# First heads' rows by way of DRAM, a rounded last key block, and a probability store in quarters

## The chip, the core and the metric

The kernel runs on one core of one Trainium2 chip. The metric is device time in microseconds (us) for one execution. A core has five engines that run their own instruction streams in order: TensorE (PE in the profile; its weight loads are PEld), VectorE (DVE), ScalarE (ACT), GpSimd (POOL) and SyncE (SP). SP here only issues DMAs, and ScalarE can issue some too. An engine goes past an instruction only when the semaphores it waits for have come, so a DMA that waits in SP's stream holds every DMA behind it.

## The reference, cut to what matters

```python
def _attn_ref(q, k, v, f):                     # (4, 8, 576, 64), f (4, 8, 576)
    scores = scale * np.matmul(q, k.transpose(0, 1, 3, 2))
    cum = np.cumsum(np.log(np.clip(f, 0.0001, 1.0)), axis=-1)
    decay = cum[:, :, :, None] - cum[:, :, None, :]
    scores = np.where(causal, -1000000000.0, scores + decay)
    attn = softmax(scores)
    return np.matmul(attn, v)

x = _attn_ref(q, k, v, f) as (2304, 512)       # heads side by side
h = np.maximum(x @ w_in, 0.0);  x = h * h @ w_out          # 512 -> 2048 -> 512
h = x @ w_in2;  out = (h - np.tanh(h)) @ w_out2            # 512 -> 2048 -> 512
```

## The kernel before, in words

There are 32 heads of 576 positions. A head's queries are cut into five tiles (64, then four of 128), its keys into five blocks of 128, 128, 128, 128 and 64. Values are kept as float32r (a rounded float32 that TensorE multiplies in one pass) in a high part and a low rest, so a product is made of two or three one-pass matmuls. A plain float32 matmul stands in the trace as two matmul instructions.

The cumulated log of `f` enters the scores as four extra rows of the contraction: rows 64 to 67 of the tile `QB`, beside the low parts of q and k. `setup` (L213) computes them (`chl`), stores them to the DRAM tensor `aug_d`, and loads the first eight heads' rows from there. The first head's rows alone go from `chl` straight to SBUF by four small DMAs of ScalarE (L245).

The heads run in four forms. `first_a` (L440) does the first 320 positions of heads 0 to 7 before any of the MLP, and takes the first weights along: `fetch_w` loads one 1 MB piece, `split_a` and `split_b` turn it into high and low float32r parts (L144 on ScalarE, L145, L146 and L122 on VectorE, L109 on ScalarE). The tables `SPLIT_A` and `SPLIT_B` say after which head which piece is split. `first_b` does the rest of these heads beside the first MLP block. Heads 8 to 15 (`attention`, L654) are transposed on TensorE. Heads 16 to 31 are laid out slot by slot by `plan_head` (L754): the probabilities are transposed in 32x32 squares by VectorE (`turn`) into `T`, stored to DRAM (`put`), loaded back in the wanted order as `PTl` (`get`), split into a high part `PTh` on ScalarE (`p_high`) and a low rest on VectorE (`p_low`), and multiplied with the values `VH` (`pv_begin`, `pv_end`). A slot is half an MLP step; in a slot, what is planned "behind" comes after the matmuls.

In `pv_parts` (L574) the key blocks 0 to 3 use the split values `VH` and split probabilities. The last 64 keys (block 4, L602) and the corner (the first 64 queries, L609) are plain float32 matmuls with the raw values `VR`.

```python
        seq = [(hi, 0), (hi, 1), (lo, 1), (hi, 2), (lo, 2), (hi, 3), (lo, 3), (None, 4), (lo, 0)]
                if pt is None:
                    nc.tensor.matmul(po4, vr[0:rows, 4], p4, start=False, stop=False)
```

The order within each engine up to the third MLP block comes from a scheduler that works by a timeline; after it, from the order in which the code is written.

Of the kernel before, what the change touches and what calls it, by code (L numbers as in the profile page):

```python
# [44 lines left out]
}  # L45
FETCH = {6: 4, 7: 5, 8: 6}
SPLIT_A = {4: 0, 6: 1, 8: 2, 9: 3}
SPLIT_B = {5: 0, 7: 1, 9: 2, 10: 3}
# [15 lines left out]
YSEQ = (0, 6, 1, 7, 2, 3, 4, 5)  # L64
PT_SZ = (64, 256, 384, 512, 576)
# [3 lines left out]
def kernel(  # L69
# [143 lines left out]
    def setup():  # L213
# [15 lines left out]
        for a in (0, 1):  # L229
            nc.vector.memset(A_QB[0][64:68, 0, a].bitcast(F32), (-1.0, 1.0)[a])  # L230
# [21 lines left out]
        for k in (0, 1, 2):  # L252
            n = min(3, H - 3 * k)
            j = int(k == 0)
            for a in (0, 1):
                queued(A_QB[k][64:68, j:, a].bitcast(F32), aug_d[3 * k + j:3 * k + n, :, a, :320].rearrange("h r s -> r h s"))
        with tc.issue_after(latest(EngineType.SP)):
            fetch_w(w1, 0, 0)
        first_load((6, 7))
        for k in (1, 2, 3):  # L260
            with tc.issue_after(latest(EngineType.SP)):
                fetch_w(w1, k, k)
# [24 lines left out]
    def load_v(u):  # L287
        VR[u] = two.tile([128, 5, D], F32, tag="VR", bufs=2, name="VR")
        src = v[u] if u < UT else v[u].rearrange("(b i) c d -> i b (c d)", b=4)
        nc.sync.dma_start(VR[u], src)  # L290

    def prep_v(u):
        VH[u] = one.tile([128, 4, 2, D], F32R, tag="VH", name="VH")
        rounded(by(pre(u) + "vh"), VH[u][:, :, 0], VR[u][:, 0:4])
        rest(by(pre(u) + "vl"), VH[u][:, :, 1], VR[u][:, 0:4], VH[u][:, :, 0])
# [28 lines left out]
    def first(h, part):  # L324
# [3 lines left out]
        if part:  # L328
            tag = ("R", "QA", "QA")[h % 3]
            r = (one if tag == "R" else two).tile([128, 2, S], F32, tag=tag, name="R0")  # L330
            vr = two.tile([128, 5, D], F32, tag="VR", bufs=2, name="VR")
# [108 lines left out]
    def first_a(also):  # L440
        st = {}
        WARM.append(psh.tile([128, 512], F32, tag="h", name="warm"))
        for h in range(H + 3):
            if h < H:
# [8 lines left out]
                if h + 3 < H:  # L453
                    with tc.issue_after(latest(EngineType.DVE)), tc.issue_after(latest(EngineType.Pool)):
                        first_prep([h + 3])
# [80 lines left out]
    def trans(u, t):  # L536
# [11 lines left out]
        if t == 1:  # L548
            rounded(by("ptr"), PT["t"][0:64, :, 3, 1], ps[0:64, 256:384].rearrange("p (q j) -> p q j", q=4))
            rounded(by("ptr"), PT["t"][0:64, 2:4, 3, 0], ps[0:64, 384:448].rearrange("p (q j) -> p q j", q=2))  # L550

    def turn(t):
        p, T = P[t], PT["t"]
        if t == 0:
            nc.vector.transpose(T[0:64, 0:2, 3, 0], p[0:64, :64].rearrange("p (b j) -> p b j", b=2))
# [7 lines left out]
    def put(u):  # L565
        by("put").dma_start(p_d[u % 2], PT["t"].rearrange("p b a s j -> p (b a s j)"))
# [7 lines left out]
    def pv_parts(u):  # L574
        vh, vr = VH.pop(u), VR.pop(u)
# [3 lines left out]
        if u < UT:  # L579
            hi, lo = (PT[k].rearrange("p q a s j -> p (q a s j)").rearrange("p (c t j) -> p c t j", c=4, t=4) for k in "hl")  # L580
            po = ps.rearrange("p (s j) -> p s j", s=4)
            at = lambda p, c, t: p[:, c, t:]
            rows = 64
            po4, p4 = ps[0:64, 384:512].rearrange("p (q j) -> p q j", q=4), PT["t"][0:64, :, 3, 1]
            po_at = lambda t: po[:, t:]
            p0 = PT["t"][0:64, 2:4, 3, 0]
        else:
            hi, lo = PT["h"], PT["l"]
            po = ps.rearrange("p (q s j) -> p q s j", q=4, s=4)
            at = lambda p, c, t: p[:, :, c, t:]  # L590
# [938 lines left out]
```

## Time and profile before

| | us |
|---|---|
| median of 3 runs (lowest to highest) | 1013.88 (1013.79 to 1014.28) |
| the profiled execution | 1015.15 |
| its span, first to last instruction | 1013.4 |
| TensorE matmuls busy, in the span | 990.9 (98%) |
| VectorE / ScalarE / GpSimd busy | 706.9 / 608.6 / 381.3 |

The profile comes from one execution. Busy time is the time that an engine has an instruction under way. A matmul that is issued and held up counts as busy, so a lengthened row shows what the idle time does not. The granted clock of TensorE is given as a share of 2.4 GHz: 1.00 and 0.50 are its two levels here.

### The profile page before, as it was taken

To read this page: it belongs to the slowest core of one execution; us is meant where nothing else is said; L and a number is where in the kernel's file an instruction comes from. 1 tells how busy PE (TensorE), PEld (TensorE's weight loads), DVE (VectorE), ACT (ScalarE), POOL (GpSimd) and SP (SyncE) were. 2 spreads that over 40 slices of the span, in tenths; PEclk is the share of its full clock that TensorE was granted. 3 is DMA by queue.
4 is the path that set the end of the run, shared out by engine and by line. 5 is a ranking of instruction groups with operands and counts; after the bars stand their busy time and mean duration, and the time that the engine had idled before them with its cause. 6 is when DMAs were issued, how large, how long until landed. Compare 5 with 4: busy or idle time off the path is not lost.

```text
span 1013.4 us, 19745 instructions
## 1 busy us (share of the span) xinstructions
PE 990.9 (98%) x7120; PEld 930.6 (92%) x7120; DVE 706.9 (70%) x1675; ACT 608.6 (60%) x1347; POOL 381.3 (38%) x453
## 2 busy tenths in 40 slices
PE   7979999999999999999999999999999999999998
PEld 7767678888999899998999999999999999999998
DVE  5886675777676777675825668477777787877851
ACT  4886676766776667676746777456556553333330
POOL 3453455555543324343402456247456520000000
PEclk8999999999999999999999999999999999999999
DMA  8545542223556556665547984997776699434451
GB/s 265 233 139 189 182 155 81 98 80 112 213 217 230 203 209 208 224 219 187 196 150 250 357 290 172 367 381 254 282 271 249 235 343 343 147 118 135 139 167 63
DMA packets 84529, 211.54 MB, mean 209 GB/s; under 512 B 8440, under 2 KB 33072, under 8 KB 80080
## 3 DMA queue, kind: packets, MB, share of 16 engines
q1 hardware_dynamic: 84304, 210.28, 59.2%
q8 instruction: 56, 0.92, 0.4%
q14 instruction: 41, 0.34, 0.1%
q10 hardware_dynamic: 128, 0.01, 0.0%
HBM read 132.20 MB, written 78.05 MB: 207 GB/s over the span
## 4 chain that ended last, share of the span: by engine, by line
PE 77%; DMA 8%; DVE 6%; ACT 3%; issue 2%; POOL 2%; SPq 1%; DVEq 0%; ACTq 0%; POOLq 0%
PE yp L193 17%; PE hp L164 17%; PE wp L1270 16%; PE wp L1194 11%; PE o_ps L605 4%; PE wp L1282 2%; DMA raw<-in_w_dram 2%; DMA R<-in_qk_dram 2%; DMA g_d<-gq 2%; PE o_ps L406 1%; DMA PTl<-p_d 1%; DVE wt L966 1%; PE s_ps L698 1%; PE t_ps L541 1%; PE s_ps L697 1%
## 5 line engine op out<-in xcount | busy, mean ns | idle before, releaser
L164 PE MATMUL hp<-xhl,w 128*128 128x288 f32 x1536 | 236.3, 299 | 2.5 <-POOL xhl L122 1.0
L164 PEld LDWEIGHTS hp<-xhl,w 128*128 128x128 f32 x1536 | 213.1, 189 | 7.8 <-issue 1.8
L193 PE MATMUL yp<-gh,w 128*128 128x288 f32 x1024 | 212.8, 299 | 0.0
L193 PEld LDWEIGHTS yp<-gh,w 128*128 128x128 f32 x1024 | 164.4, 188 | 3.1 <-issue 2.1
L1194 PE MATMUL wp<-xo,wg 128*128 128x288 f32 x1152 | 159.9, 296 | 2.0 <-DVE gq L1201 1.9
L1270 PE MATMUL wp<-go,wg 128*128 128x256 f32 x1344 | 161.4, 283 | 0.0
L1270 PEld LDWEIGHTS wp<-go,wg 128*128 128x128 f32 x1344 | 161.4, 192 | 0.0
L1194 PEld LDWEIGHTS wp<-xo,wg 128*128 128x128 f32 x1152 | 155.0, 188 | 3.5 <-DVE gq L1201 3.4
L193 PE MATMUL yp<-gl,w 128*128 128x288 f32 x512 | 151.5, 297 | 0.0
L517 POOL TENSOR_SCALAR P<-P,ST 128x448 f32<-128x448 f32 (+4 forms) x120 | 83.4, 704 | 136.6 <-DVE ST L713 83.0
L109 ACT ACTIVATE go<-gt 128x1792 fp32r<-128x1792 f32 (+1 forms) x34 | 58.3, 1717 | 101.2 <-PE wp L1270 79.9
L497 DVE CUSTOM_DVE_ANT_0 P<-s_ps,mk 128x320 f32<-128x320 f32 (+3 forms) x151 | 63.5, 438 | 72.6 <-PE s_ps L698 41.5
L506 ACT ACTIVATE P<-P,ST 128x320 f32<-128x320 f32 (+4 forms) x151 | 84.8, 562 | 47.3 <-DVE ST L497 45.2
L193 PEld LDWEIGHTS yp<-gl,w 128*128 128x128 f32 x512 | 96.4, 188 | 0.8 <-issue 0.8
L122 DVE TENSOR_TENSOR gl<-tmp,gh 128x288 fp32r<-128x288 f32 x96 | 58.6, 611 | 51.6 <-ACT tmp L174 51.1
L122 DVE TENSOR_TENSOR go<-gt,go 128x1792 fp32r<-128x1792 f32 (+1 forms) x34 | 69.6, 2048 | 34.9 <-ACT go L109 32.0
L170 ACT ACTIVATE tmp<-hp 128x288 f32<-128x288 f32 x128 | 52.0, 406 | 63.1 <-PE hp L164 62.2
L122 POOL TENSOR_TENSOR wt<-wt,whi 128x512 f32<-128x512 f32 (+1 forms) x48 | 60.7, 1286 | 59.2 <-ACT whi L109 28.8
L174 ACT ACTIVATE tmp<-tmp 128x288 f32<-128x288 f32 x128 | 56.7, 443 | 3.4
L173 ACT ACTIVATE gh<-tmp 128x288 fp32r<-128x288 f32 x128 | 56.1, 438 | 1.9
L1201 DVE TENSOR_TENSOR gq<-wp,sm 128x288 f32<-128x288 f32 x96 | 40.8, 453 | 17.0 <-ACT sm L1200 11.3
L1245 DVE TENSOR_TENSOR gt<-gt 128x256 f32<-128x256 f32 x128 | 49.4, 428 | 1.5 <-DMA gt<-g_d 0.4
(171 smaller groups left out, 1673.7 us busy)
## 6 DMA issues: line engine op xcount, KB each, us to landing
wg<-wg_d SPq DMA_DIRECT2D x24, 896.0 KB
g_d<-gq SPq DMA_DIRECT2D x32, 576.0 KB
raw<-in_w_dram SPq DMA_DIRECT2D x16, 1024.0 KB
p_d<-T SPq DMA_DIRECT2D x16, 1024.0 KB
PTl<-p_d SPq DMA_DIRECT2D x64, 256.0 KB
raw<-in_w_dram SPq DMA_DIRECT2D x32, 512.0 KB
gt<-g_d SPq DMA_DIRECT2D x32, 512.0 KB
R<-in_qk_dram SPq DMA_DIRECT2D x24, 576.0 KB
```

The source lines that it names most:

```text
L109: eng.activation(out, in_, AF.Copy)
L122: eng.tensor_tensor(out, in_, hi.bitcast(F32), ALU.subtract)
L164: nc.tensor.matmul(ps, w[:, k * 128:(k + 1) * 128], x[:, k], start=(jj == 0), stop=(jj == 11))
L170: nc.scalar.activation(tmp, ps, AF.Relu)
L173: nc.scalar.activation(gh, tmp, AF.Square)
L174: nc.scalar.activation(tmp, tmp, AF.Square)
L193: nc.tensor.matmul(yp[m][:, :n], w[:, c], x, start=(at == 0 and j == 0), stop=(at == NF - 1 and j == 2))
L497: nc.vector.tensor_tensor_reduce(p[:rows, a:b], ps[:rows, :b - a], mk[:rows, o:o + b - a], -0.125, 3.0e38 if mn is None else mn, ALU.add, ...
L506: nc.scalar.activation(p[:rows, :n], p[:rows, :n], AF.Exp, bias=mn, scale=-1.0, accum_out=st[:rows, 1, t:t + 1])
L517: by(n_by).tensor_scalar(p[:rows, :n], p[:rows, :n], st[:rows, 3, t:t + 1], 1.0, ALU.mult, ALU.mult)
L1194: nc.tensor.matmul(ps, wg[:, ws, k * 128:(k + 1) * 128], xo[:, xs, k], start=(i == 0 and first_), stop=(i == 5), skip_group_check=True)
L1270: nc.tensor.matmul(ps, wg[:, ws, m * 128:(m + 1) * 128], YO[n][xs][:, YX[xn]], start=(j == 0 and m == 0 and i == 0), stop=(j == 2 and i == ...
```

## The change

Six things are edited. (1) The extra rows of head 0 are no longer written to SBUF directly: `chl` is stored to `aug_d` by two DMAs of ScalarE instead of SyncE, and the rows of heads 0 to 2, 3 to 5 and 6 to 7 are loaded from there, each group in front of a weight piece. (2) `SPLIT_A` and `SPLIT_B` split the first weight pieces after earlier heads. (3) Block 4 of the keys is split like the others (`VH` has five blocks), and so is the corner. (4) The raw values have one buffer instead of two, loaded after the values of the head before are split. (5) `put` stores four quarters of 512 columns. (6) `get` is planned one slot earlier, behind the matmuls.

```diff
-    "ptr": "V", "pth": "A", "ptl0": "V", ...
+    "pth": "A", "pth3": "A", "ptl0": "V", ...
-SPLIT_A = {4: 0, 6: 1, 8: 2, 9: 3}
-SPLIT_B = {5: 0, 7: 1, 9: 2, 10: 3}
+SPLIT_A = {1: 0, 4: 1, 7: 2, 9: 3}
+SPLIT_B = {2: 0, 5: 1, 8: 2, 10: 3}
+LOW = (0, 0, 0, 1)
@@ setup
-        for r in (0, 1):
+        nc.scalar.dma_start(aug_d[:, 0:2, 0], chl.bitcast(F32))
+        nc.scalar.dma_start(aug_d[:, 2:4, 1], chl.bitcast(F32))
+        def aug(k, put):
+            n = min(3, H - 3 * k)
             for a in (0, 1):
-                p = 64 + 2 * a + r
-                nc.scalar.dma_start(A_QB[0][p:p + 1, 0, a].bitcast(F32), chl[0:1, r, :320].bitcast(F32))
-        queued(aug_d[:, 0:2, 0], chl.bitcast(F32))
-        queued(aug_d[:, 2:4, 1], chl.bitcast(F32))
+                put(A_QB[k][64:68, :, a].bitcast(F32), aug_d[3 * k:3 * k + n, :, a, :320].rearrange("h r s -> r h s"))
         first_load((4,))
+        aug(0, queued)
+        early(0)
...
+        aug(1, queued)
         first_load((5,))
...
@@ load_v, prep_v
-        VR[u] = two.tile([128, 5, D], F32, tag="VR", bufs=2, name="VR")
+        VR[u] = two.tile([128, 5, D], F32, tag="VR", bufs=1, name="VR")
-        VH[u] = one.tile([128, 4, 2, D], F32R, tag="VH", name="VH")
+        VH[u] = one.tile([128, 5, 2, D], F32R, tag="VH", name="VH")
@@ trans
-            rounded(by("ptr"), PT["t"][0:64, :, 3, 1], ps[0:64, 256:384].rearrange("p (q j) -> p q j", q=4))
-            rounded(by("ptr"), PT["t"][0:64, 2:4, 3, 0], ps[0:64, 384:448].rearrange("p (q j) -> p q j", q=2))
+            rounded(nc.scalar, eh, ps[0:64, 256:448])
+            rest(nc.vector, el, ps[0:64, 256:448], eh)
@@ put
-        by("put").dma_start(p_d[u % 2], PT["t"].rearrange("p b a s j -> p (b a s j)"))
+        for b in range(4):
+            by("put").dma_start(p_d[u % 2][:, 512 * b:512 * b + 512], PT["t"][:, b].rearrange("p a s j -> p (a s j)"))
@@ pv_parts
-        seq = [(hi, 0), (hi, 1), (lo, 1), (hi, 2), (lo, 2), (hi, 3), (lo, 3), (None, 4), (lo, 0)]
-        if u >= UT:
-            seq = [(hi, 0), (hi, 1), (hi, 2), (hi, 3), (None, 4), (lo, 1), (lo, 2), (lo, 3), (lo, 0)]
+            seq = [(hi, 0), (hi, 1), (lo, 1), (hi, 2), (lo, 2), (hi, 4), (hi, 3), (lo, 3), (lo, 4), (lo, 0)]
+            seq = [(hi, 0), (hi, 1), (hi, 2), (hi, 3), (hi, 4), (lo, 1), (lo, 2), (lo, 3), (lo, 4), (lo, 0)]
-            nc.tensor.matmul(ps0[0:64, 0:64], vr[0:rows, 0], p0, start=True, stop=True)
+            for n, (a, p) in enumerate(((0, hi), (1, hi), (0, lo))):
+                nc.tensor.matmul(ps0[0:64, 0:64], vh[0:rows, 0, a], p0(p), start=(n == 0), stop=(n == 2))
@@ p_high, p_low
-        s0 = max(0, c - 1)
+        s0 = LOW[c]
@@ plan_head
-            plan(o + 7, get, k)
+            plan(o + 6, get, k, behind=True)
```

At the start, SyncE's stream before (`R` is a head's raw q and k, `V` the values, `raw` a weight piece) was:

```order
L211 DMA R_135<-in_qk_dram 128x2x320
L211 DMA aug_d<-chl 32x2x576 x2
L211 DMA R_166<-in_qk_dram 128x2x320
L211 DMA V_168<-in_v_dram 128x8x192
L211 DMA R_166<-in_qk_dram 128x2x320
L211 DMA QB_142<-aug_d 4x2x320 x2
L211 DMA QB_143<-aug_d 4x3x320 x2
L211 DMA QB_144<-aug_d 4x2x320 x2
L134 DMA raw<-in_w_dram 128x2048
```

and is now:

```order
L212 DMA R_135<-in_qk_dram 128x2x320
L212 DMA R_160<-in_qk_dram 128x2x320
L338 DMA R_728<-in_qk_dram 64x1152
L212 DMA QB_142<-aug_d 4x3x320 x2
L135 DMA raw<-in_w_dram 128x2048
L212 DMA V_166<-in_v_dram 128x8x192
L212 DMA QB_143<-aug_d 4x3x320 x2
L212 DMA R_160<-in_qk_dram 128x2x320
L135 DMA raw<-in_w_dram 128x2048
```

The `chl` stores have left SyncE, the first weight piece has moved up from behind all the rows to right behind those of the first three heads.

ScalarE's stream in the same stretch (`QA<-R` are heads 0, 1 and 2, then more; `P,ST` is an exponential of head 0) was:

```order
L109 ACTIVATE QA_188<-R_132 128x640 x2
L109 ACTIVATE QA_197<-R_135 128x640
L245 DMA QB_142<-chl 1x16x20 x4
L265 ACT_TABLE_LOAD
L265 ACTIVATE wrk<-wrk 32x1
L109 ACTIVATE QA_197<-R_135 128x640
L109 ACTIVATE QA_291<-R_166 128x640 x2
L506 ACTIVATE P_241,ST<-P_241,ST 128x320
```

and is now:

```order
L110 ACTIVATE QA_182<-R_132 128x640 x2
L110 ACTIVATE QA_191<-R_135 128x640
L267 ACT_TABLE_LOAD
L267 ACTIVATE wrk<-wrk 32x1
L241 DMA aug_d<-chl 32x2x576
L242 DMA aug_d<-chl 32x2x576
L145 ACTIVATE raw<-raw 128x1024
L512 ACTIVATE P_235,ST<-P_235,ST 128x320
```

The stores stand behind the table load, and the first step on the first weight piece stands in front of head 0's first exponential, where three heads' `QA` stood.

In a head of the last form that closes a pair, SyncE's stream was:

```order
L566 DMA p_d_83<-T 128x2048
L489 DMA x_d_81<-xsh 128x576
L490 DMA x_d_81<-xs 128x576
L572 DMA PTl<-p_d_83 32x4x512 x4
L269 DMA R<-in_qk_dram 128x1152
```

and is now:

```order
L572 DMA p_d_83<-T 128x512 x4
L578 DMA PTl<-p_d_83 32x4x512 x4
L495 DMA x_d_81<-xsh 128x576
L496 DMA x_d_81<-xs 128x576
L271 DMA R<-in_qk_dram 128x1152
```

The load of `PTl` has moved ahead of the two stores of the attention output, and there are four stores of a quarter each. Load b waits for the store of quarter b.

## Rows read from the trace of the kernel before

**Rows 1.** The page, busy time of each engine in the span.

```profile
PE 990.9 (98%) x7120; PEld 930.6 (92%) x7120; DVE 706.9 (70%) x1675; ACT 608.6 (60%) x1347; POOL 381.3 (38%) x453
```

**Rows 2.** TensorE in order of time, a head of the last form: start, length, line, operation.

```profile
264.78 0.43 PE L193 MATMUL yp<-gh,w 128*128 128x288 f32 x2
...
266.40 0.91 PE L605 MATMUL o_ps<-PTh,VH 128*128 128x512 f32 x4
267.24 0.43 PE L602 MATMUL o_ps<-PTl,VR 128*64 128x128 f32 x2
267.60 1.85 PE L164 MATMUL hp<-xhl,w 128*128 128x288 f32 x12
269.29 0.92 PE L605 MATMUL o_ps<-PTl,VH 128*128 128x512 f32 x4
...
270.39 0.53 PE L193 MATMUL yp<-gh,w 128*128 128x288 f32 x2
```

**Rows 3.** TensorE in order of time, a head of the form before it.

```profile
172.18 0.28 PE L605 MATMUL o_ps<-PTl,VH 128*128 128x256 f32 x1
...
172.75 0.49 PE L605 MATMUL o_ps<-PTl,VH 128*128 128x512 f32 x1
...
173.43 1.85 PE L164 MATMUL hp<-xhl,w 128*128 128x288 f32 x12
```

**Rows 4.** TensorE in order of time, the smallest float32r matmuls there are.

```profile
276.72 0.21 PE L697 MATMUL s_ps<-QA 128*128 128x64 f32 x1
276.77 0.28 PE L698 MATMUL s_ps<-QB 68*128 68x64 f32 x1
276.88 0.51 PE L164 MATMUL hp<-xhl,w 128*128 128x288 f32 x2
```

**Rows 5.** TensorE in order of time, the first and last of eight lengthened groups.

```profile
298.67 1.43 PE L605 MATMUL o_ps<-PTh,VH 128*128 128x512 f32 x4
...
470.41 1.58 PE L605 MATMUL o_ps<-PTh,VH 128*128 128x512 f32 x4 [0.86 <-issue]
```

**Rows 6.** SyncE's queue in order of time, a head that closes a pair.

```profile
283.96 0.34 SPq L566 DMA_DIRECT2D p_d<-T  x1
...
289.79 2.54 SPq L572 DMA_DIRECT2D PTl<-p_d  x4
```

**Rows 7.** The chain that ended last, 385 to 422 us: start, length, what.

```profile
404.13 3.88 DMA p_d<-T
...
409.99 6.43 DMA PTl<-p_d
```

**Rows 8.** ScalarE in order of time, the high part of one head's `PTl`.

```profile
280.19 1.88 ACT L109 ACTIVATE PTh<-PTl 128x512 fp32r<-128x512 f32 x4 [1.06 <-DMA PTl<-p_d]
```

**Rows 9.** The start in order of time: VectorE, ScalarE's queue, ScalarE.

```profile
2.59 0.57 DVE L231 TENSOR_SCALAR wrk<-wrk 32x576 f32<-32x576 f32 x1 [1.06 <-DMA wrk<-in_f_dram]
7.51 2.69 ACTq L245 DMA_DIRECT2D QB<-chl  x4
10.23 1.28 ACT L265 ACT_TABLE_LOAD   x1 [1.99 <-DVE QB L113]
17.44 0.55 ACT L506 ACTIVATE P<-P,ST 128x320 f32<-128x320 f32 x1
```

**Rows 10.** The chain that ended last, its first 16 us.

```profile
0.74 0.40 SPq L218
...
7.51 3.09 DMA QB<-chl
10.61 4.66 DMA R<-in_qk_dram
```

**Rows 11.** Busy time by stretch: length, PE, PEld, DVE, ACT, POOL, granted clock, DMA share.

```profile
17.00:27.00 10.00, 9.52 (x43) 9.10 (x43) 6.03 (x31) 5.30 (x21) 1.45 (x5) 0.50 0.98 380
...
49.80:56.00 6.20, 3.87 (x20) 2.41 (x20) 4.69 (x5) 6.02 (x12) 2.90 (x4) 1.00 0.24 32
...
67.80:71.00 3.20, 0.10 (x2) 0.05 (x1) 2.56 (x8) 1.56 (x4) 3.14 (x5) 1.00 0.02 8
```

More of the change, by code (lines that the diff above doesn't have):

```diff
@@ L241, in setup, with early @@
         nc.vector.scalar_tensor_tensor(chl[:, 1], cum, 8.0, chl[:, 0].bitcast(F32), ALU.mult, ALU.subtract)
-        for r in (0, 1):
+        nc.scalar.dma_start(aug_d[:, 0:2, 0], chl.bitcast(F32))
+        nc.scalar.dma_start(aug_d[:, 2:4, 1], chl.bitcast(F32))
+        def aug(k, put):
+            n = min(3, H - 3 * k)
             for a in (0, 1):
-                p = 64 + 2 * a + r
-                nc.scalar.dma_start(A_QB[0][p:p + 1, 0, a].bitcast(F32), chl[0:1, r, :320].bitcast(F32))
-        queued(aug_d[:, 0:2, 0], chl.bitcast(F32))
-        queued(aug_d[:, 2:4, 1], chl.bitcast(F32))
+                put(A_QB[k][64:68, :, a].bitcast(F32), aug_d[3 * k:3 * k + n, :, a, :320].rearrange("h r s -> r h s"))
+        def early(k):
+            with tc.issue_after(latest(EngineType.SP)):
+                fetch_w(w1, k, k)
         first_load((4,))
+        aug(0, queued)
+        early(0)
         A_V[0] = slot_pool(11).tile([128, H, 3, D], F32, tag="w11", name="V0")
         queued(A_V[0].rearrange("p h c d -> p h (c d)"), v[0:H, :, :3].rearrange("h p c d -> p h (c d)"))
+        aug(1, queued)
         first_load((5,))
[L252 to L258, printed above, removed]
+        early(1)
+        aug(2, queued)
         first_load((6, 7))
-        for k in (1, 2, 3):
-            with tc.issue_after(latest(EngineType.SP)):
-                fetch_w(w1, k, k)
+        early(2)
+        early(3)
         with tc.issue_after(latest(EngineType.DVE)):
@@ L330, in first @@
             r = (one if tag == "R" else two).tile([128, 2, S], F32, tag=tag, name="R0")
-            vr = two.tile([128, 5, D], F32, tag="VR", bufs=2, name="VR")
+            if h % 2:
+                vr = one.tile([128, 5, 2, D], F32, tag="VH", name="V0").rearrange("p c a d -> p (c a d)")[:, :5 * D].rearrange("p (c d) -> p c d", c=5)
+            else:
+                vr = two.tile([128, 5, D], F32, tag="VR", bufs=1, name="VR")
             nc.sync.dma_start(r[0:64], qk[h][0:64])
@@ L453, in first_a @@
                 if h + 3 < H:
-                    with tc.issue_after(latest(EngineType.DVE)), tc.issue_after(latest(EngineType.Pool)):
+                    with tc.issue_after(latest(EngineType.DVE)), tc.issue_after(latest(EngineType.Pool)), tc.issue_after(latest(EngineType.Activation)):
                         first_prep([h + 3])
@@ L548, in trans @@
         if t == 1:
-            rounded(by("ptr"), PT["t"][0:64, :, 3, 1], ps[0:64, 256:384].rearrange("p (q j) -> p q j", q=4))
-            rounded(by("ptr"), PT["t"][0:64, 2:4, 3, 0], ps[0:64, 384:448].rearrange("p (q j) -> p q j", q=2))
+            eh, el = (x[0:64, 3].rearrange("p t j -> p (t j)")[:, :192] for x in (PTh, PTl))
+            rounded(nc.scalar, eh, ps[0:64, 256:448])
+            rest(nc.vector, el, ps[0:64, 256:448], eh)
     def turn(t):
@@ L574, in pv_parts @@
     def pv_parts(u):
-        vh, vr = VH.pop(u), VR.pop(u)
+        vh = VH.pop(u)
         b, h = divmod(u, H)
@@ L638, in pv @@
         products, corner, upper, out = pv_parts(u)
-        products(0, 9)
+        products(0, 10)
         corner()
@@ L672, in attention @@
                     prep_v(p)
+                if t == 3 and u0 - 1 <= p:
+                    load_v(p + 1)
             if p + 3 < NU:
@@ L718, in p_high @@
     def p_high(c):
-        s0 = max(0, c - 1)
-        rounded(by("pth"), PT["h"][:, :, c, s0:], PT["l"][:, :, c, s0:].bitcast(F32))
+        s0 = LOW[c]
+        rounded(by("pth3" if c == 3 else "pth"), PT["h"][:, :, c, s0:], PT["l"][:, :, c, s0:].bitcast(F32))
     def p_low(c):
-        s0 = max(0, c - 1)
+        s0 = LOW[c]
         lo = PT["l"][:, :, c, s0:]
@@ L747, in pv_end @@
     def pv_end(u):
-        PV[u][0](5, 9)
+        PV[u][0](5, 10)
         PV[u][1]()
```

33 lines of the change are left out of this document (13 added, 20 removed), and 2 rows, old and new, of the table ENG.

## The prediction

> **What bounds the kernel now.** The busy times come first: TensorE is busy for 990.9 of 1013.4 us [rows 1], so nearly all of the span is TensorE's own work, and a change pays in three ways: less work on TensorE, fewer of the waits that hide inside lengthened matmuls, or less of the idle 22 us. The second view is TensorE in order of time, in one head of the last form (16 heads) and one of the form before it (8 heads) [rows 2, 3]: the attention's matmuls stand between the MLP's without a gap, but the plain float32 pairs take long. The third is the same view searched for lengthened groups: the four matmuls on `PTh` that take 0.91 us in one head [rows 2] take up to 1.58 in eight heads [rows 5]. What they wait for is read from SyncE's queue and from the chain [rows 6, 7]. The last is the start, where the chain, the queues and the busy time by stretch show a late first score, ten microseconds at the lower clock and two holes [rows 9 to 11].
>
> **TensorE's work on the last key block and the corner.** First the rate: 12 MLP matmuls of 288 columns go from 264.78 to 266.40 [rows 2], 0.135 us each, so 1664 columns (512+512+384+256) are worth 0.78. In the last form the high group lasts from 266.40 to 267.60, so 1.20-0.78 = 0.42 goes to the float32 pair of block 4 with the pause before it; the low group lasts from 269.29 to 270.39, and 1.10-0.78 = 0.32 goes to the corner's pair. Sum 0.74 a head. In the form before, the 256 columns at 172.18 are worth 0.12 and the next one-pass matmul starts at 172.75: 0.45 for block 4; 512 columns from 172.75 are worth 0.24 and the next starts at 173.43: 0.44 for the corner [rows 3]. Sum 0.89. In their place come five one-pass matmuls, two of 128 columns and three of 64. No one-pass matmul of 128 columns is in the trace; the nearest rows are two of 64, which start 0.05 and 0.11 before the next [rows 4]. I take 0.08 each, their mean, since matmuls of this size seem to be set by loading the weights: five cost 0.40, with ends of 0.25 and 0.55. The last form saves 0.34 a head (0.19 to 0.49), the form before 0.49 (0.34 to 0.64). **16 x 0.34 + 8 x 0.49 = 9.4 us** (5.8 to 13.0). All of it is on the path, since TensorE has no other cover there.
>
> **The round trip through DRAM.** Eight groups exceed the usual 0.92 [rows 2], the first by 0.51 and the last by 0.66 [rows 5], 4.44 in all, and before two of them TensorE stands idle, for 0.86 [rows 5] and 0.35: 5.65 us. Each waits for `PTh`, which waits for the four loads of `PTl`, which wait for the store. In a head that closes a pair the store is issued at 283.96 and the first load at 289.79, behind two stores of the output that are not ready [rows 6]; elsewhere the load follows when the store has landed, 3.88 later, and the last load lands 6.43 after its issue [rows 7]. Planned one slot earlier and behind the matmuls, the load stands ahead of the output's stores, which gives a closing head about 5.8-3.9 = 1.9 us. Quarters land earlier than the whole: no store of a quarter is in the trace. The smallest load there, 72 KB of `f` (L218), was issued at 0.74 [rows 10] and its reader ran at 2.59 [rows 9], 1.85; the whole megabyte took 3.88. I take 2.5 for the first quarter, nearer to the small one. The four loads take 2.54 to issue, one after the other [rows 6], so the last quarter, issued some 1.0 later, is in time: every head gains 1.4. Against that, `PTh` and `PTl` grow from 1664 to 1920 columns a partition: 1.88 x 0.154 = 0.29 more on ScalarE [rows 8], ahead of the waiting matmul, and about as much on VectorE, behind it. Even heads gain 1.1 net, closing heads 3.0; the waits were at most 0.66+0.86 = 1.52. So most of it goes: **4.8 of 5.65 us** (0 to 5.65). What is moved past the load on SyncE's queue, the output's two stores, the next q and k and its rows, is not wanted for most of a head; if the load blocks the queue longer than a head, they are late next.
>
> **The start.** The four DMAs of ScalarE take 2.69 us to issue from 7.51, 0.67 each, and the table load that follows takes 1.28 [rows 9]. Now the table load comes first: ScalarE's work before it ends at 10.23-1.99 = 8.24, so the two stores are issued at about 9.6 and 10.3. A store and a load after it land in 1.85 each at best [rows 9, 10] and in 3.09 each by the row of the four small DMAs [rows 10]: the first score moves from 15.3 (10.61+4.66 [rows 10]) to somewhere between 14.2 and 16.5. I take no change. Then a new wait: ScalarE's first exponential stands behind the first step on the first weight piece, and VectorE's second row minimum behind its own step. The piece, 1 MB, is issued at about 13 and lands 3.9 to 6.4 later [rows 7], and the step takes 1024 x 1.88/1664 = 1.16 [rows 8]. The first exponential comes at 18.1 to 20.6 instead of 17.44 [rows 9]; I take 18.6, +1.2, near the lower end, since little else is then on the queues. Queued behind it are the second head's exponentials and the third `QA`; the first transposes wait. On the other side, work that was done late is done early. From 49.8 to 56 ScalarE is busy for 6.02 of 6.20 us and TensorE for 3.87 [rows 11]: of two weight steps ahead of the last head's output one is left, about -1.1. From 67.8 to 71 TensorE does nothing [rows 11] and waits for a normalisation that began behind VectorE's weight steps; three fewer stand ahead of it, of which TensorE's own work just before takes back the greater part: -1 (0 to -3). The clock stood at 0.50 from 17 to 27 [rows 11], which costs half of ten microseconds; it may fall later, not at all (-5) or stay down longer (+2.5 for five more). Sum: **-1 us** (-8 to +5).
>
> **Costed at nothing.** The copies of block 4 to the store's tile go (two on VectorE a head) and one on ScalarE and one on VectorE come; the value split grows from four blocks to five. ScalarE stands at 60% and VectorE at 70% of the span [rows 1], and both wait for TensorE's scores in each head; without that cover they cost under 0.5 us a head, 12 us in all. One buffer for the raw values costs nothing as long as the split precedes the load by most of a head, which the order shows. Three more DMA instructions a head are SyncE's, which issues a store in 0.34 [rows 6].
>
> **The sum.** -9.4 - 4.8 - 1 = -15.2. Against the profiled execution (span 1013.4, 1015.15 in all) that is 1000.0; that execution was 1.3 above the median of 1013.88, and against the median it is 998.7. I forecast 999; the ends of the three terms (3.6, about 2 and 6 to either side) hardly meet, and half of their sum gives its own range, 993 to 1005.
>
> **Weighed against the skill.** The trace shows a one-megabyte store that lands 3.88 us after its issue [rows 7]. The Trainium skill, "DMA: Bandwidth & Descriptors", section "Measured (HBM→SBUF, 128 partitions, SWDGE, issued from GpSimd)", says to batch transfers to 1 MiB or more to get three quarters of the peak rate, which speaks against quarters. The same page's fit in "Anatomy of one DMA" (2.0 us and the bytes at 436 GB/s) gives an estimate of 4.4 us for the whole and 2.6 for a quarter, so by the fit the first quarter comes 1.8 earlier and the sum hardly moves; the rule would have the four together last longer than the one, which is the second rival below.
>
> **The rivals.** *The saving on TensorE turns into waits.* If scores, exponential, normalisation and transposition of a head already last as long as TensorE's work between them, TensorE waits for what it no longer does. For it: VectorE at 70%, and lengthened groups as the sign that a margin is small. Against it: eight of sixteen heads of the last form show no lengthening. Price: the whole 9.4, so 1013.9-4.8-1 = 1008.
>
> *The quarters land no sooner than the whole.* Then every head's wait stays as it is, except that closing heads gain 1.9, and the chain through `PTh` is 0.29 longer. For it: the loads must wait for the values' low products in any case, and the 6.43 of the last load [rows 7] is a matter of traffic, which quarters don't lessen. Taking no gain and 0.29 more in eight heads: 1013.9-9.4-1+2.3 = 1006.
>
> *The start gets worse.* The piece lands at the late end (+3.2) and the clock stays down for five more microseconds (+2.5), and the two holes stay: 1013.9-9.4-4.8+5.7 = 1005.
>
> *Slower than before.* One mechanism: TensorE, held up again and again by VectorE and ScalarE as they wait for weight pieces, never gets its clock back before 49.8. What it does from 27 to 49.8, 22.8 us, would take twice as long: 1013.9-9.4-4.8+22.8+1.2 = 1024. It decides the sign once it costs over 14 us. Against it: the clock came back at 27 with TensorE busy for 9.52 of 10 [rows 11], and the warming matmuls are still in the order.
>
> **How the numbers follow.** Forecast 0.60; waits in place of the saving 0.14; quarters no sooner 0.15; a worse start 0.08; slower 0.03. The predicted time is the forecast's, 999. The range holds its own 993 to 1005, the third and second rivals, and on the lower side the upper bounds of the saving: 992 to 1008, which leaves out the slow case and about half of the first. A measurement of this kernel tells a change from none at about 0.2%, 2 us: faster 0.95, within that 0.02, slower 0.03.
>
> **What would show it.** In the trace after, a high group of the last form followed by the MLP should last 0.86 (five matmuls) and a low group with its corner about 1.1. If these last 1.2 and more, the small matmuls were priced too low. No group on `PTh` should last over 1.1; if several do, the round trip has not shortened, and the time from the first store to the first load says why. The first score should stand near 15, the first exponential between 18 and 21. The clock by stretch tells whether the low stretch has moved. If TensorE's matmuls are shorter and its idle time is longer by as much, the first rival is right. What would make the forecast wrong altogether is a loss in the first 70 us greater than 14.

## The result

| | us |
|---|---|
| before, median of 4 runs (lowest to highest) | 1014.08 (1013.79 to 1015.37) |
| changed, median of 4 runs | 1005.88 (1005.07 to 1006.66) |
| changed to before | 0.9917, 95% interval 0.9899 to 0.9934 |
| span of the profiled execution, before and changed | 1013.4 and 1004.5 |

The change gains 8.2 us. The forecast was 999, a gain of 15; the result lies inside the range and outside the forecast's own 993 to 1005. So one question decides: where are the other 6 to 7 us?

Busy times of the changed kernel (the page), beside [rows 1]:

```profile
PE 981.3 (98%) x7144; PEld 933.9 (93%) x7144; DVE 717.7 (71%) x1665; ACT 614.0 (61%) x1355; POOL 396.4 (39%) x452
```

TensorE is busy for 9.6 us less, and the span is 8.9 shorter. Where that came from is read by landmarks: the same instruction found in both traces. Here they are the scores of 448 columns (one for each head from the ninth on), the first product of the second MLP (`wp`) and the last row of matmuls.

| stretch | before | changed | difference |
|---|---|---|---|
| start to the first 448-column scores | 137.9 | 135.6 | -2.3 |
| two heads, the crossing from the first heads to the next form | 30.5 | 32.8 | +2.3 |
| seven heads of the form before the last | 90.2 | 91.9 | +1.7 |
| from there to the last form | 15.6 | 16.0 | +0.4 |
| thirteen heads of the last form | 221.6 | 209.8 | -11.8 |
| rest of the first MLP | 147.1 | 146.1 | -1.0 |
| second MLP | 366.2 | 367.8 | +1.6 |

The gain lies in the last form. The form before it, of which 3.9 us were expected, has become slower.

**The last form.** TensorE in order of time, the head that answers to [rows 2]:

```profile
268.91 0.97 PE L607 MATMUL o_ps<-PTh,VH 128*128 128x512 f32 x5
269.72 0.48 PE L165 MATMUL hp<-xhl,w 128*128 128x288 f32 x2
...
271.37 1.03 PE L607 MATMUL o_ps<-PTl,VH 128*128 128x512 f32 x5
272.23 0.25 PE L612 MATMUL o_ps<-PTh,VH 128*64 128x64 f32 x2
...
272.38 0.51 PE L194 MATMUL yp<-gh,w 128*128 128x288 f32 x2
```

From the high group to the MLP it is 0.81 us (1.20 before), from the low group through the corner 1.01 (1.10 before): 0.48 a head. Of the eight lengthened groups of [rows 5] one is left, the longest row on `PTh`; the others last 0.97 to 0.99:

```profile
347.90 1.81 PE L607 MATMUL o_ps<-PTh,VH 128*128 128x512 f32 x5
```

SyncE's queue in a head that closes a pair, beside [rows 6]: the first load follows the first store by 2.2 us (5.8 before), and the output's stores stand behind it. In four of the sixteen heads it is 2.7 to 3.5, in the first 4.6.

```profile
285.87 1.81 SPq L572 DMA_DIRECT2D p_d<-T  x4
288.08 3.53 SPq L578 DMA_DIRECT2D PTl<-p_d  x4
291.66 0.59 SPq L495 DMA_DIRECT2D x_d<-xsh  x1
```

**The form before it.** TensorE in order of time, a head's corner and the end of its products, beside [rows 3], and then the end of the same head's products before:

```profile
184.87 0.30 PE L612 MATMUL o_ps<-PTh,VH 64*64 64x64 f32 x2
...
185.15 0.40 PE L165 MATMUL hp<-xhl,w 128*128 128x288 f32 x1
...
185.80 0.34 PE L607 MATMUL o_ps<-PTl,VH 128*128 128x384 f32 x1
186.07 0.64 PE L607 MATMUL o_ps<-PTh,VH 64*128 64x128 f32 x2
186.55 0.97 PE L607 MATMUL o_ps<-PTl,VH 128*128 128x256 f32 x3
187.35 1.34 PE L165 MATMUL hp<-xhl,w 128*128 128x288 f32 x9
```
```profile
185.98 0.34 PE L605 MATMUL o_ps<-PTl,VH 128*128 128x384 f32 x1
...
186.49 0.43 PE L602 MATMUL o_ps<-T,VR 64*64 64x128 f32 x2
186.85 0.49 PE L605 MATMUL o_ps<-PTl,VH 128*128 128x512 f32 x1
187.18 1.09 PE L164 MATMUL hp<-xhl,w 128*128 128x288 f32 x7
```

In a row of several matmuls the shape is that of the first. From the product of 384 columns (185.80) the order is: block 4 high (64 rows), block 3 high, block 3 low, block 4 low (64 rows), block 0 low, MLP. That takes 1.55 us, and its 1664 columns are worth 0.78 at the MLP's rate. The same stretch before, with the plain pair, took 1.20 (185.98 to 187.18). The corner takes 0.28 (0.25 before). Together a head has 1.83 where it had 1.45: **0.38 more, where 0.49 less was forecast**. Over eight heads that is 6.9 us, as much as is missing.

**The start.** The chain that ended last, then TensorE and ScalarE in order of time:

```profile
7.21 5.56 DMA aug_d<-chl
```
```profile
15.31 0.39 PE L375 MATMUL s_ps<-QB 68*128 68x320 f32 x1 [2.77 <-DMA QB<-aug_d]
23.32 0.48 PE L374 MATMUL s_ps<-QA 128*128 128x320 f32 x1 [2.83 <-DVE ST L503]
141.50 0.30 PE L549 MATMUL t_ps<-ident,P 128*64 128x128 f32 x1 [1.94 <-POOL P L523]
```
```profile
19.50 0.56 ACT L512 ACTIVATE P<-P,ST 128x320 f32<-128x320 f32 x1
```

The first score comes at 15.31 as before, the first exponential at 19.50 (17.44 before), behind the step on the weight piece (which landed at 18.41), and TensorE then waits 2.83 us for VectorE. Busy times by stretch (length, PE, PEld, DVE, ACT, POOL, granted clock, DMA share, GB/s), the stretches of [rows 11] and two more:

```profile
17.00:27.00 10.00, 7.17 (x34) 6.59 (x34) 8.18 (x32) 8.27 (x24) 2.75 (x5) 0.68 1.06 349
49.80:56.00 6.20, 6.04 (x34) 3.79 (x32) 4.08 (x6) 5.31 (x14) 3.84 (x5) 1.00 0.01 1
57.00:61.00 4.00, 3.38 (x14) 3.38 (x15) 4.00 (x5) 3.33 (x7) 2.50 (x2) 0.57 0.75 177
67.80:71.00 3.20, 1.83 (x14) 1.60 (x14) 3.04 (x4) 1.65 (x4) 3.14 (x4) 1.00 0.38 154
140.00:150.00 10.00, 8.50 (x52) 8.22 (x53) 6.07 (x22) 7.09 (x20) 5.62 (x9) 0.83 0.51 172
```

Both holes have shrunk (TensorE busy for 6.04 of 6.20, 3.87 before, and for 1.83 of 3.20, 0.10 before). The granted clock is 0.68 from 17 to 27 us (0.50 before) and falls once more at 57 to 61. At 139.6 TensorE waits 1.94 for a normalisation that stands on GpSimd behind a step of 2 us on `QB`. That transposition came at 143.71 before, so the lead of 2.2 us still holds at 141.50; it is gone by 168.4, and here the clock falls in between (0.83 from 140 to 150).

### The profile page after: what moved, and what is told of

It reads as the page before. It is cut to its first block, busy times and chain, and to the rows that moved or that the text cites. A ratio compares the mean times of both kernels' runs of the same rounds, so it can differ in the third digit from the quotient of the medians.

```text
span 1004.5 us, 19864 instructions
## 1 busy us (share of the span) xinstructions
PE 981.3 (98%) x7144; PEld 933.9 (93%) x7144; DVE 717.7 (71%) x1665; ACT 614.0 (61%) x1355; POOL 396.4 (39%) x452
## 4 chain that ended last, share of the span: by engine, by line
PE 73%; DVE 9%; DMA 8%; ACT 4%; issue 2%; SPq 1%; POOL 1%; DVEq 0%; ACTq 0%; POOLq 0%
PE wp L1272 16%; PE yp L194 15%; PE hp L165 15%; PE wp L1196 12%; PE o_ps L607 4%; PE wp L1284 2%; DMA g_d<-gq 2%; PE o_ps L412 1%; DMA raw<-in_w_dram 1%; DMA PTl<-p_d 1%; DVE PTl L123 1%; DMA p_d<-T 1%; DVE wt L968 1%; PE t_ps L547 1%; ACT P L512 1%
## 5 line engine op out<-in xcount | busy, mean ns | idle before, releaser
L523 POOL TENSOR_SCALAR P<-P,ST 128x448 f32<-128x448 f32 (+4 forms) x120 | 95.8, 807 | 136.5 <-DVE ST L715 76.3
L1334 POOL TENSOR_TENSOR gq<-sm,sm 128x288 f32<-128x288 f32 x32 | 28.6, 894 | 56.3 <-ACT sm L1333 35.0
```

Of the source, the lines that this page charges most:

```text
L523: by(n_by).tensor_scalar(p[:rows, :n], p[:rows, :n], st[:rows, 3, t:t + 1], 1.0, ALU.mult, ALU.mult)
```

## Experiments

The ratio behind each time is to the runs of the kernel before that were measured beside it; over the three series these spread from 1009.5 to 1019.2 us, with medians of 1013.0 to 1014.6. Differences of 1 to 3 us between two experiments are therefore read from their stretches, not from their times.

The theory after the comparison: a product of 64 contraction rows among products of 128 rows costs a pause before and behind it. The plain pair was one such place in a head, the rounded products are two. The rival: each small matmul has a price of its own, whatever its rows. Stretch and corner below are the two stretches read above (1.55 and 0.28 in the changed kernel).

**Block 4 in one place, and block 4 with all rows.** e1_pair:

```diff
-  ..., (lo, 2), (hi, 4), (hi, 3), (lo, 3), (lo, 4), (lo, 0)]
+  ..., (lo, 2), (hi, 3), (lo, 3), (hi, 4), (lo, 4), (lo, 0)]
```

> One edit to the changed kernel: in the heads of the form before the last (8 heads), the two products of block 4 (64 rows of contraction among products of 128 rows) stand next to each other, behind those of block 3. In the changed kernel's trace the stretch from the product of 384 columns at 185.80 to the MLP at 187.35 is 1.55 us, and its 1664 columns are worth 0.78. Theory, a pause where the rows change: each run of 64-row matmuls costs a pause before and behind it, and two such runs become one, so the stretch falls to about 1.2 and 8 heads give 2 to 3 us: 1003. Rival, each small matmul has a price of its own: the same matmuls in another order, the stretch stays at 1.55 and the time at 1005.9.

e2_full_rows (the values' rows below 64 in block 4 are zero already):

```diff
-  at = lambda p, c, t: p[0:64, 3, 0] if c == 4 ...
-  p0 = lambda p: p[0:64, 3, 1, :64]
-  rows = 64
+  at = lambda p, c, t: p[:, 3, 0] if c == 4 ...
+  p0 = lambda p: p[:, 3, 1, :64]
+  rows = 128
@@ steady_init, for PTh and PTl
+  nc.gpsimd.memset(x[64:128, 3, 0:2].bitcast(F32), 0.0)
```

> One edit to the changed kernel: in the 8 heads of the form before the last, block 4 and the corner contract over 128 rows, of which the lower 64 hold zeros, so no product of the values has 64 rows. The columns stay the same. Theory, a pause where the rows change: the pauses go, the stretch of 1.55 falls to 0.8 to 0.9 and the corner's three products from 0.28 to 0.15, so a head falls by 0.8 and the kernel by 6 to 7 us: 999. Rival, each small matmul has a price of its own: no change, 1005.9. Second rival, the saving is there but this form's heads wait for exponential and normalisation instead: the stretch is short, the period of a head stays at 13.3, and the time is above 1004.

TensorE in order of time, the end of a head's products in e1_pair, then in e2_full_rows:

```profile
186.77 0.35 PE L607 MATMUL o_ps<-PTl,VH 128*128 128x384 f32 x1
...
187.28 0.32 PE L607 MATMUL o_ps<-PTh,VH 64*128 64x128 f32 x1
187.44 0.70 PE L607 MATMUL o_ps<-PTl,VH 64*128 64x128 f32 x2
187.98 1.35 PE L165 MATMUL hp<-xhl,w 128*128 128x288 f32 x9
```
```profile
184.20 0.34 PE L607 MATMUL o_ps<-PTl,VH 128*128 128x384 f32 x1
184.38 0.39 PE L607 MATMUL o_ps<-PTh,VH 128*128 128x128 f32 x2
184.61 0.63 PE L607 MATMUL o_ps<-PTl,VH 128*128 128x256 f32 x3
185.07 1.34 PE L165 MATMUL hp<-xhl,w 128*128 128x288 f32 x9
```

The same matmuls in another order: 1.21 us instead of 1.55. With 128 rows: 0.87, and the corner 0.15 (three starts at 196.51 to 196.66). The rival has fallen: neither the number nor the columns of the matmuls changed. With 128 rows stretch and corner are 1.02, 0.43 less than before the change, close to the 0.49 that was forecast for both forms. As times: 1004.88 (ratio 0.9897, 0.9864 to 0.9931) and 1002.73 (0.9885, 0.9845 to 0.9924). That is less than the stretches gained. Seven heads take 90.8 and 88.3 us (91.9); had the 0.8 a head of e2_full_rows come through whole, it would be 86 there. The waits of TensorE from 150 to 262 us in e2_full_rows (us in all, times, longest) say why:

```profile
PE s_ps L536 <- DVE xs L625: 2.3, 5, 0.8
```

The changed kernel has no such wait. The second rival in e2_full_rows's expectation is in part right: part of the saving turned into a wait for a free bank (the piece of memory that TensorE writes a product to, here one that VectorE has yet to empty).

**The pause by itself.** e7_probe appends series of matmuls (the time is longer by them).

> The changed kernel with eight series of 24 rounds of matmuls appended at its end, whose results nobody reads, so the total is longer by their length. A round is: 256 columns at 128 rows; 128 columns at 128 rows; 128 columns at 64 rows; then 256 columns at 128 rows followed by 128 columns at 128 rows, by 128 at 64 rows, by two of 128 at 64 rows, by a plain float32 of 128 columns at 128 rows, by such a one at 64 rows. Theory, a pause where the rows change: 0.12 and 0.06 to 0.08 for the single kinds at either height, 0.18 to 0.20 for 256+128 at 128 rows, 0.4 to 0.6 for 256+128 at 64 rows, and only 0.06 to 0.08 more with the second one at 64 rows. Rival, a price for each small matmul: 256+128 takes the same at 64 and at 128 rows, and the second one at 64 rows costs as much as the first. The plain float32 one: 0.45 to 0.55 at 128 rows by the pair of the last form before, and by the pause another 0.2 to 0.3 at 64 rows.

TensorE in order of time, at the full clock: 256 columns with 128 columns at 128 rows, 256 with 128 at 64 rows, 256 with a plain float32 of 128 columns at 128 rows and at 64 rows.

```profile
1016.21 0.34 PE L1490 MATMUL wp<-a,a 128*128 128x256 f32 x1
1016.38 0.22 PE L1491 MATMUL wp<-a,a 128*128 128x128 f32 x1
1016.44 0.34 PE L1490 MATMUL wp<-a,a 128*128 128x256 f32 x1
...
1017.42 0.38 PE L1493 MATMUL wp<-a,a 128*128 128x256 f32 x1
1017.74 0.32 PE L1494 MATMUL wp<-a,a 64*128 64x128 f32 x1
1017.99 0.39 PE L1493 MATMUL wp<-a,a 128*128 128x256 f32 x1
...
1071.43 0.38 PE L1501 MATMUL wp<-a,a 128*128 128x128 f32 x2
1071.57 0.36 PE L1500 MATMUL wp<-a,a 128*128 128x256 f32 x1
...
1074.97 0.49 PE L1504 MATMUL wp<-a,a 64*128 64x128 f32 x2
1075.38 0.38 PE L1503 MATMUL wp<-a,a 128*128 128x256 f32 x1
```

A round takes 0.23, 0.57, 0.34 (1071.23 to 1071.57) and 0.73 us (1074.65 to 1075.38). The same 128 columns cost 0.06 at 128 rows and 0.40 at 64: the pause is 0.34. The plain one costs 0.39 more at 64 rows. Three points missed. 128 columns alone took 0.11 at either height, where 0.06 to 0.08 was expected. The plain one at 128 rows was expected at 0.45 to 0.55, so the 0.42 of the last form was not the pair alone. And the series with two products of 64 rows ran at the lower clock as a whole (1.13 a round against 0.91 with one at that clock), so the second one costs 0.22 there, the first 0.59 (0.91 less the 0.32 of the 256 columns); 0.06 to 0.08 was expected for the second.

One thing stays open. The plain pair of the last form before contracts over 128 rows, but its weights have 64 columns (128*64), and it takes 0.36 us (267.24 to 267.60 [rows 2]), as long as the pair of 64*64 above (186.49 to 186.85); with 128 columns of weights the probe's pair takes 0.14 (1071.43 to 1071.57). The three rounded products of 128*64 take 0.15 in all (272.23 to 272.38). So plain products show a cost beside fewer weight columns as well, and part of the 0.48 that the last form saved may be its removal; no run separates the two.

The Trainium skill has the rule, "TensorEngine Tiling (Array Packing)", section "Key Properties": a change of the tiling mode drains TensorE. By the same page's "Available Configurations", 64 rows by 128 columns is another mode than 128 by 128. It gives no price. The runs with rounded products of 64 rows agree with it, if these products select that mode, which no trace says: 0.34 us for going there and back. The rounded products of 128*64, by that list a mode of their own too, show no such pause (0.15 for three). The scores on `QB` contract over 68 rows and show no pause (0.11 [rows 4]).

**The parts of the round trip.** e5_whole_store undoes the quarters, e6_late_get the earlier load:

```diff
@@ e5_whole_store, put
-  for b in range(4):
-      by("put").dma_start(p_d[u % 2][:, 512 * b:512 * b + 512], PT["t"][:, b]...)
+  by("put").dma_start(p_d[u % 2], PT["t"].rearrange("p b a s j -> p (b a s j)"))
@@ e6_late_get, plan_head
-  plan(o + 6, get, k, behind=True)
+  plan(o + 7, get, k)
```

> The changed kernel with one undone: the probabilities of a head are stored whole (1 MB) and not in quarters; the load of PTl stays where the change put it. In the changed kernel the first load is issued 2.2 us after the first store in most heads (3.3 in the slowest), 3.9 after the whole store before, and one of 16 groups on PTh is lengthened (1.81 against 0.97). Theory, the quarters shorten the round trip by 1.4 to 1.7 in every head and that is what removed the waits: several groups on PTh last over 1.1 again, 2 to 4 us in all, time 1008 to 1010. Rival, the earlier place in SyncE's queue did it: one or two lengthened groups as now, time within 1 us of 1006.

> The changed kernel with the other half undone: quarters stay, but the load of PTl is planned a slot later, where it was before, behind the output's stores in heads that close a pair. Theory, quarters alone are enough in heads that do not close a pair, and closing heads wait again for the output's stores: the load comes 4 to 6 us after the first store there, up to eight lengthened groups, 1 to 3 us in all, time 1007 to 1009. Rival, quarters alone do it everywhere: no group over 1.1 beside the one that is there, time within 1 us of 1006.

e5_whole_store: 1008.92 (ratio 0.9956, 0.993 to 0.9982), thirteen heads in 212.8 us (209.8). Seven groups on `PTh` are over 1.05, the longest first; over 0.97 each they hold 3.3 us. e6_late_get: 1011.48 (0.9967, 0.9946 to 0.9989), thirteen heads in 215.1; seven groups, in every second head, those that close a pair, hold 4.8 us, and TensorE is idle for 0.5. One row of each:

```profile
282.92 1.85 PE L606 MATMUL o_ps<-PTh,VH 128*128 128x512 f32 x5
```
```profile
399.68 1.81 PE L607 MATMUL o_ps<-PTh,VH 128*128 128x512 f32 x5 [0.50 <-ACT PTh L110]
```

SyncE's queue in e6_late_get, for the head of that last row:

```profile
384.90 1.79 SPq L572 DMA_DIRECT2D p_d<-T  x4
...
388.63 0.33 SPq L495 DMA_DIRECT2D x_d<-xsh  x1
...
390.56 3.69 SPq L578 DMA_DIRECT2D PTl<-p_d  x4
```

The first theory holds in both, in e6_late_get with more than the 1 to 3 us that it gave, and the place in the queue is worth more than the quarters. With the quarters undone 3.3 us of waits are left, with the place undone 5.3, of 5.65 before. That one part alone leaves so much fits with heads that are 0.48 shorter on TensorE, so that less stands ahead of the products; had only block 4 been changed, most of its saving might have turned into these waits, but no run shows that.

**The start.** e4_old_start takes the setup and tables of the kernel before; e3_late_split only the tables. (The change had also put `first_prep`, which prepares a head's q and k, behind ScalarE's latest instruction in the order; e4_old_start takes that back too.)

```diff
@@ e3_late_split
-SPLIT_A = {1: 0, 4: 1, 7: 2, 9: 3}
-SPLIT_B = {2: 0, 5: 1, 8: 2, 10: 3}
+SPLIT_A = {4: 0, 6: 1, 8: 2, 9: 3}
+SPLIT_B = {5: 0, 7: 1, 9: 2, 10: 3}
@@ e4_old_start: the same, and setup() and the place of first_prep as before
```

> The changed kernel with the start of the kernel before (rows of the first head straight from ScalarE, the other rows by SyncE, first weight pieces split after the old heads); block 4, corner, quarters and the earlier load as changed. In the changed kernel the first scores of the form before the last come at 133.81 (136.54 before), and then a hole of 1.94 us at 139.6 and a stretch at the lower clock give back 3.3. Theory, both belong to the start: the scores come at 136.5 again and the hole and the low clock go, so the time is 1005.9 + 2.7 - 3.3, about 1005. Rival, the hole belongs to the new products of that form and stays: 1005.9 + 2.7, about 1008.6.

> The changed kernel with the two tables SPLIT_A and SPLIT_B as before, the rows and the first weight piece still loaded in the new order. In the changed kernel TensorE waits 2.8 us at 20.5 for VectorE, which stands behind its step on the first piece, and the first scores of the attention come at 121.23 (123.67 before). Theory, the early pieces come from the early load, and the tables only shift the steps by a head: the first scores of the attention within 0.5 us of 121.2, the time within 1 us of 1006. Rival, the tables are what takes the work out of the stretch from 50 to 70 us: without them the two holes there are back as before (2.3 and 3.1 us), the scores come at 123 to 124 and the time is 1008.

e4_old_start: 1008.55 (0.9939, 0.9918 to 0.996), the 448-column scores at 137.9 as before. Against the changed kernel's 135.6 the new start is worth 2.3 us there; in the eight other traces with this start they come at 133.5 to 137.3, so one trace tells it only to some 2 us. The crossing takes 31.7, between 30.5 and 32.8, so the theory that all of its loss belongs to the start falls; the rival's time came out. e3_late_split: 1002.9 (0.9887, 0.9847 to 0.9928), the first attention scores at 121.25 as the theory says, but 3 us faster than it says: 448-column scores at 133.3 and a crossing of 31.3. The tables of before, with the new loads, look better; the intervals overlap, and below they gave nothing.

**Once more, and one part undone.** e12_old_form gives the form before the last its plain pair back (`VR` and `T` as before the change), the rest as changed.

> The changed kernel itself, once more, beside the three below on the same chip. Both theories: 1004.5 to 1007.5. Its trace tells what belongs to one execution: in the first one TensorE's clock was at 0.83 from 140 to 150 us, and the second MLP took 367.8 us from its first product to the last matmul (366.2 before). In six traces of the same order of those stretches the clock fell after 140 in two and the second MLP took 367.1 to 369.9; if both come out otherwise here, they are chance and not the change.

> The changed kernel with one part undone: in the 8 heads of the form before the last, block 4 and the corner are plain float32 products with the raw values, as before the change; the last form keeps the rounded ones. In the changed kernel the period of these heads is 13.2 to 13.4 us, 12.9 to 13.0 before. Theory, the rounded products of 64 rows cost more than the plain pair that they replaced, since they stand in two places: the period is 12.9 to 13.0 again, and the kernel is 2.5 to 3 us faster than the changed one, 1003. Rival, these heads are longer for another reason (the raw values with one buffer, ScalarE's and VectorE's new steps): the period stays at 13.2 to 13.4 and the time at 1006.

The changed kernel again: 1006.98 (0.9927, 0.9904 to 0.9951). Its clock does not fall after 140, and its crossing takes 32.8 all the same, with a wait for VectorE's row minimum (0.75) in place of the low clock. The low clock stands in four of nine traces with this start (changed, e2_full_rows, e6_late_get, e7_probe), so the loss at the crossing does not need it. The second MLP takes 367.1 there. e12_old_form: 1005.84 (0.9913, 0.9882 to 0.9944). Its products last as before the change, 1.20 (197.14 to 198.34) and 0.26. But seven heads take 91.4 us, not 90.2, the time is the rival's, and there is a new wait from 160 to 262 us:

```profile
PE o_ps L609 <- ACT PTh L110: 1.9, 4, 0.6
```

ScalarE waits more for VectorE's row minimum there: 16.6 us in all from 160 to 262, the longest 2.5 (12.3 and 1.4 before). This mixture keeps the old copies on VectorE and has the new fifth block of values too, which may be why. So the undoing shows the length of the products and not their worth in time.

**A faster version.** e8_one_bank adds to e2_full_rows the scores of the two smallest tiles in one bank:

```diff
@@ scores, t == 1
+  ps = bank(u, "s_ps")
+  for k, c in ((1, 0), (0, 192)):
+      o = ps[:, c:c + NKEY[k]]    # products of tile k, then row_min and soften of both
```

> The kernel with 128-row products in the form before the last (e2_full_rows) and one more edit: in that form the scores of the two smallest query tiles (192 and 64 columns) go to one PSUM bank instead of two. In e2_full_rows TensorE waits five times, 2.3 us in all, at the 64-column scores for VectorE's addition that empties the bank of the output before (L625). Theory, the saving on TensorE turned into a wait for a free bank: with a bank less to take, that wait goes and nothing takes its place, so the time is about 2 us under e2_full_rows, 1000 to 1001. Rival, VectorE is late as a whole there: the same wait appears at the next bank that TensorE takes, and the time is that of e2_full_rows, 1002 to 1003.

> The three edits that gained, together: products of 128 rows and scores in one bank in the form before the last, and the two SPLIT tables as before. Theory, they are in different stretches and add up: e8_one_bank was 6.5 us under the changed kernel and e3_late_split 3.0, so 996 to 997. Rival, e3_late_split gained at the crossing from the first heads to the attention (133 to 146 us), where e8_one_bank had gained too (its crossing took 11.4 us instead of 13.3): then some 2 us less, 998 to 999.

> The kernel e9_late_one_bank, and the plain float32 products of 64 rows in the first eight heads (one in each of their two parts) contract over 128 rows too, the lower ones zero (16 small memsets more on VectorE). In the appended series a round with a plain product of 64 rows took 0.73 us at the full clock, one of 128 rows 0.34, so each such product costs 0.39 more. Theory, the eight of the second part are on the path: 3 us, and those of the first part, where TensorE waits for others, nothing: 993 to 994. Rival, TensorE waits for VectorE and GpSimd in these stretches and waits longer instead: within 1 us of e9_late_one_bank.

e8_one_bank: **999.39** (0.9841, 0.9799 to 0.9884), faster than both kernels. From 150 to 262 us the wait for the bank is down to one, of 0.8 us. Seven heads take 85.5 us, 6.4 less than in the changed kernel, and the crossing 30.7. e9_late_one_bank (e8_one_bank with the tables of before): 999.92 (0.9847, 0.9812 to 0.9883), nothing more. The theory falls. The rival, that both gain at the crossing, is nearer, but its 998 to 999 did not come out either: the crossing is 30.1, the scores come 0.8 later than in e8_one_bank (136.1), and the second MLP is the longest of all (370.9). e10_first_rows, the same and 128 rows in the first eight heads: 999.88 (0.9858, 0.9821 to 0.9894), nothing: the 448-column scores come at 135.6 (136.1 without), and TensorE waits 1.9 us for a copy of ScalarE in the first heads and 4.6 for VectorE's row minimum (2.8 without). The products did get shorter: in the second part a plain pair with its two neighbours takes 0.66 where it took 0.94. So its rival is right: where TensorE waits for others, its pauses cost nothing.

## Why the prediction was right in kind and wrong in size

**The step that failed** is the price of the small matmuls, "I take 0.08 each, their mean, since matmuls of this size seem to be set by loading the weights". It was taken from rows of 128 and 68 rows [rows 4] and used for both forms. In the last form block 4 and the corner contract over 128 rows, and it was even too high: the saving is 0.48 a head and not 0.34, 7.7 us for sixteen and not 5.4. In the form before they contract over 64 rows, and there a head got 0.38 slower instead of 0.49 faster: +3.0 us and not -3.9. The sum of that step is -4.7 and not -9.4, below its range (5.8 to 13.0). The traces of e1_pair, e2_full_rows and e7_probe show the cause: for the rounded products it is the change of rows, 0.34 us each time, and not their size. What I should have seen: the pair that stands between the rows of [rows 3] contracts over 64 rows, and a pause beside it is part of its 0.45. The pair's cost was read as the cost of plain float32, which the change removes; part was the cost of 64 rows, which it keeps and doubles. (That the last form's pair of 128 rows cost nearly as much, 0.42, is the point left open above.)

**The round trip**: 4.8 us forecast, 4.8 measured (5.65 less the 0.84 that is left). The first quarter was taken to land 2.5 us after its issue; the first load follows the first store by 2.2 us in most heads (2.7 to 3.5 in four, 4.6 in the first). The growth of `PTh` is 0.2 (2.08 at 297.42, 1.88 before). The Trainium skill's fit in "DMA: Bandwidth & Descriptors", "Anatomy of one DMA", made 2.6 of it, an estimate for DMAs that GpSimd issues; its rule to batch into 1 MiB spoke against quarters, and e5_whole_store, 3 us slower, decides against the rule at this place.

**The start**: -1 forecast, -2.3 measured at 135.6, nothing left at 168.4. The first score was right for a wrong reason. The stores were issued at 7.21 and 7.59, ahead of the table load (7.95), not behind it at 9.6; but the first landed 5.56 us after its issue, not 1.85 to 3.09. The first exponential came 0.9 later than taken, within its bounds. Both holes shrank as said, and the low clock of the first 27 us, which the sum had left as it was, shrank too (0.68 for 0.50). Not foreseen was the crossing, where the lead is lost after 141.5: one trace has the low clock there, the other waits of 1.0 us for VectorE, and 0.4 is the crossing's own head with 64 rows. What makes up the rest, and what VectorE is late with, was not tried.

**The rivals.** The saving turned into waits in part, in the form before the last (2.3 us in e2_full_rows), and in the last form waits of 3.3 and 5.3 us come back when a part of the round trip's gain is undone. The quarters did land sooner. The clock fell at 57 to 61 and cost less than 2 us.

**Not in the prediction**: the second MLP, 1.6 us longer, in code that was not touched. TensorE waits for `gq`, which VectorE writes only when an earlier store of it has landed (VectorE waits 3.82 us for that at 660.72, 2.4 at the longest before):

```profile
PE wp L1196 <- DVE gq L1203: 2.2, 2, 1.8
```

These waits came to 1.9 us in four before, so they alone do not make the 1.6. Behind the longest the granted clock is at 0.50 from 661.8 to 665.1 us; before, it stays at 1.00. The DMA engines are as full as before (share 1.00 from 630 to 660, 1.01 from 640 to 670 before). In the twelve other traces of this study the stretch takes 366.9 to 370.9 us. It was shortest in the kernel before (366.2); whether an earlier begin or chance makes it longer stays open.

Together: the forecast's 15.2, less 4.7 for the small matmuls, 0.6 for the start and the crossing (-0.4 in place of -1, the crossing's own head with 64 rows left out) and 1.6 for the second MLP, and 1.0 more for waits on a bank that stood in these heads before and are gone, make 9.3; the traces differ by 8.9.

## What to carry to other kernels

Price a small matmul by a row with the same rows and columns of the array and the same precision, not by its columns alone: a rounded one of 64 rows among those of 128 cost 0.34 us more here, and filling it up to 128 rows with zeros took that away. If products with few rows can't be filled up, put them next to each other. Before a saving on the bounding engine is booked, look at what else must come earlier for it: here the bank that VectorE empties (3.3 us, e8_one_bank against e2_full_rows) and the load behind SyncE's stores (5.6, e6_late_get against the changed kernel) were each worth as much as the products of 64 rows (3.2, e2_full_rows).

## What was not expected of the hardware

Beside the pause of 0.34 us: TensorE's clock fell to the lower level while its matmul rows show no idle time. In e7_probe, by stretch (columns as above):

```profile
1017.00:1020.00 3.00, 3.00 (x13) 1.88 (x11) 0.00 (x0) 0.00 (x0) 0.00 (x0) 1.00 0.00 0
1020.20:1036.60 16.40, 16.40 (x37) 10.22 (x36) 0.00 (x0) 0.00 (x0) 0.00 (x0) 0.51 0.00 1
1066.00:1074.00 8.00, 8.00 (x64) 8.00 (x63) 0.00 (x0) 0.00 (x0) 0.00 (x0) 0.86 0.01 2
```

Before it fell, TensorE alternated between 128 and 64 rows since 1016.9 (it had fallen once before, in the series of 64 rows alone, and come back); it stayed at 1.2 GHz through both such series and rose to 2.4 GHz at about 1068, in the series of plain products at 128 rows; it fell again at 1078.4, in that of plain products at 64 rows. So matmul rows without idle time were no sign there that the clock would stay up. In the kernels' own heads with 64 rows (150 to 260 us) it stayed at 1.00.
